# Token chunks of 128 for the second mixer's value products, and one early load of w_sg

## The chip, the cores and the metric

The kernel runs on one core of one Trainium2 chip. The metric is device time in microseconds (us); before the change the median of three runs is 643.07 us (642.69 to 643.32). Names used below: PE is TensorE (matrix products), PEld the loading of its stationary operand ("weights"), DVE VectorE, ACT ScalarE, POOL GpSimd, SP the engine whose queue issues nearly all DMAs.

## The reference, cut to what matters

Two batches of 448 tokens with 768 channels pass through attention and two mixers. The change is in the second mixer, on whose input x it computes:

```python
h = x @ w_in                                   # 768 -> 1024
h = 0.5 * h * (1 + np.tanh(c * (h + 0.044715 * h ** 3)))
u, v = h[..., :512], h[..., 512:]
v_n = (v - mean(v)) / np.sqrt(var(v) + 1e-06) * g_ln      # over channels
v_s = np.einsum('ts,bsd->btd', w_sg, v_n) + b_sg[None, :, None]
return x + (u * v_s) @ w_out
```

The einsum mixes tokens: w_sg is 448 by 448, and the same for both batches. Before it stands the first mixer, a Fourier mix and a wide MLP (768 to 3072 to 768).

## The kernel before, in words

Every product that needs more than bf16 precision is done with operands split in a high and a low half (helper `split`: ACT copies the high half, DVE subtracts to get the low one), and three matrix instructions per block of 128 contracted rows: high by high, high by low, low by high. The helper `product` issues these, so one line, L140, holds nearly all of PE's work, and it is told apart by tiles: h and c are the first and second product of the MLP, u and v those with the two halves of w_in, sg the token mix with w_sg, out the product with w_out.

The MLP runs in six groups g = 0 to 5 of 512 hidden channels. In a group, h is computed for batch 0 and batch 1 (72 instructions each), then c for batch 0 and batch 1. Each group needs eight weight tiles, w1_(4g) to w1_(4g+3) and w2_(4g) to w2_(4g+3). They come as float64 words through one SP queue into two raw buffers (tag `raw`, 768 KB each), and ACT and DVE turn each into a high and a low half in about seven instructions. The trace leaves the digits before the underscore out: w_8 is w1_8 as well as w2_8. Tiles w1_4 and w1_5 lie in a pool of their own, `wc`, which is closed when group 1's h products have been written down.

From group 1 on a scheduler sets the order on each engine: it takes instructions of all program parts as their inputs are expected, so that parts written one after another are interleaved, and then each engine runs its list strictly in that order.

Products with one result of up to 512 columns take their PSUM bank from `one_ps`, a ring of four banks. So the c product that is four places later waits for the DVE to have read the earlier one.

w_sg is needed transposed and split, as sgT. Before, this is done in group 3 (L1145 to L1152): four tiles of 112 rows each are loaded into one buffer, one after another (`bufs=1`), transposed on PE in four pieces of 112 by 112, and split. The tokens are thus in four chunks of 112 (CP = 112, NT = 4).

After the last group follow u for batch 0, v for batch 0, u for batch 1, sg for batch 0, v for batch 1, out for batch 0, sg for batch 1, out for batch 1. `gate_values` computes v: for each chunk of 112 tokens the tokens are the stationary operand (128 contracted rows by 112 columns) and 256 columns of w_in stream past; 36 instructions a chunk, 144 a batch. Each chunk then goes through the tanh form of gelu, a norm over its 512 channels, and a split into vn. `gate` contracts the chunks of vn with sgT: four chunks, three instructions each, for each of four blocks of 128 channels.

Of the kernel before, what the change touches and what calls it, by code (L numbers as in the profile page):

```python
# [21 lines left out]
P = 128  # L22
# [2 lines left out]
NP = H // 2  # L25
CP = S // 4
NT = 4
FF1 = 4 * C
NF = FF1 // P
NG = 6  # L30
# [60 lines left out]
def attention_mixers_kernel(ctx, tc, bounded, q, k, v, cap, w_ch1, w_ch2, w_in, g_ln, w_sg, b_sg, w_out,  # L91
# [76 lines left out]

    xT = [keep.tile([P, NP, S], F32, name=f"xT{b}") for b in range(B)]
    normed = [None, None]  # L170


    def fourier(b, fp, t2sb, pool_folds=()):
# [83 lines left out]
    def layer_norm(b, fp):  # L257

        u = xT[b]

        def channel_sum(half, src, tag):
            vec.tensor_tensor(half, src[0], src[1], op=ALU.add)
            acc = fp.tile([P, S], F32, tag="acc", name=f"acc_{tag}{b}")
            vec.tensor_tensor(acc, half[:, 0, :], half[:, 1, :], op=ALU.add)
            vec.tensor_tensor(acc, acc, half[:, 2, :], op=ALU.add)
            return acc

        t = SimpleNamespace(d=[], sq=[])

        def total():  # L270
            half = fp.tile([P, 3, S + 2], F32, tag="y", bufs=2, name=f"half{b}")[:, :, :S]
            t.acc = channel_sum(half, (u[:, 0:3, :], u[:, 3:6, :]), "m")

        def mean():
            t.mu = two_ps(f"mu{b}", 1)[0]
            pe.matmul(t.mu[:, :S], mean_w, t.acc, start=True, stop=True)

        def centre():
            for i in range(2):
                d = fp.tile([P, 3, S], F32, tag="d", bufs=2, name=f"d{b}_{i}")  # L280
                vec.tensor_tensor(d, u[:, 3 * i:3 * i + 3, :], t.mu[:, :S].unsqueeze(1).to_broadcast([P, 3, S]),
                                  op=ALU.subtract)
                t.d.append(d)

        def square():
            for i in range(2):
                q2 = fp.tile([P, 3, S + 2], F32, tag="y", bufs=2, name=f"sq{b}_{i}")[:, :, :S]
                act.activation(q2, t.d[i], AF.Square)
                t.sq.append(q2)

        def square_total():
            t.acc2 = channel_sum(t.sq[0], t.sq, "v")

        def variance():
            t.vps = two_ps(f"var{b}", 1)[0]
            if bounded and not b:
                stream(t.vps, 12)
            for i in range(NT):
                pe.matmul(t.vps[:CP, 2 * i:2 * i + 2], t.acc2[:, i * CP:(i + 1) * CP], mean_w[:, 0:2],
                          start=True, stop=True)  # L300

        def deviation():
            var = small.tile([CP, NT], F32, tag="var", name=f"varc{b}")
            vec.tensor_scalar(var, t.vps[:CP, 0:2 * NT:2], 1e-6, None, op0=ALU.add)
            t.rstd = small.tile([CP, NT], F32, tag="rstd", name=f"rstd{b}")
            pool.tensor_tensor(t.rstd, var, neg_half[:CP, :NT], op=ALU.pow)

        def row():
            t.rps = two_ps(f"rstdrow{b}", 1)[0]
            if bounded and b:  # L310
                stream(t.rps, 12)
            for i in range(NT):
                pe.matmul(t.rps[:, i * CP:(i + 1) * CP], t.rstd[:, i:i + 1].to_broadcast([CP, P]), ident[:CP, :CP],
                          start=True, stop=True)

        def scale(c):
            part = lambda c: t.d[c // 3][:, c % 3, :]
            if c == 0:
                un[b] = normed[b].tile([P, 2, NP, S], F32R, tag="normed", name=f"un{b}")
            if c < NP:  # L320
                vec.tensor_tensor(part(c), part(c), t.rps[:, :S], op=ALU.mult)
            if 0 < c <= NP:
                act.copy(un[b][:, 0, c - 1, :], part(c - 1))
            if c > 1:
                vec.tensor_tensor(un[b][:, 1, c - 2, :], part(c - 2), f32(un[b][:, 0, c - 2, :]), op=ALU.subtract)  # L325

        return SimpleNamespace(total=total, mean=mean, centre=centre, square=square, square_total=square_total,
                               variance=variance, deviation=deviation, row=row, scale=scale)
# [466 lines left out]
    def gate_values(b, gp, x2, wv):  # L795

        vn = []

        def normalise(t, gv, mv):
            tc.keep_in_program_order(  # L800
                vec.tensor_scalar(gv, gv, mv[:, 0:1], mv[:, 1:2], op0=ALU.subtract, op1=ALU.mult))
            w = hpool[b].tile([P, 2, 512], F32R, tag="h", bufs=4, name=f"vn{b}_{t}")[:CP]
            split(w[:, 0], w[:, 1], gv)
            vn.append(w)

        last = None
        for t in range(NT):
            ps = one_ps(f"v{b}_{t}")
            for j in range(2):
                product(ps[:CP, j * 256:(j + 1) * 256], lambda n, a: x2[:, a, n, t * CP:(t + 1) * CP],  # L810
                        lambda n, a: wv[2 * j + n // 3][:, a, n % 3, :], NP)
            gv = gp.tile([P, DH], F32, tag="gv", bufs=3, name=f"gv{b}_{t}")[:CP]
            gelu2(gp, gv, ps[:CP, :], CP, f"v{b}_{t}", last)
            st = small.tile([P, 6], F32, tag="bst", name=f"bst{b}_{t}")[:CP]
            vec.bn_stats(st, gv)
            mv = small.tile([P, 2], F32, tag="bag", name=f"bag{b}_{t}")[:CP]
            vec.bn_aggr(mv, st)

            vec.tensor_scalar(mv[:, 1:2], mv[:, 1:2], 4e-6, None, op0=ALU.add)  # L819
            pool.tensor_tensor(mv[:, 1:2], mv[:, 1:2], neg_half[:CP, 0:1], op=ALU.pow)  # L820
            last = functools.partial(normalise, t, gv, mv)
        last()
        return vn
# [11 lines left out]
    def gate(b, gp, vn, ug, sgT, g_half, b_half):  # L835
        gated = normed[b].tile([P, 2, ND, S], F32R, tag="normed", name=f"gated{b}")
        for d in range(ND):
            ps = one_ps(f"sg{b}_{d}")
            product(ps[:, :S], lambda n, a: vn[n][:, a, d * P:(d + 1) * P], lambda n, a: sgT[:, a, n, :], NT)
            tmp = gp.tile([P, S], F32, tag="gelu", bufs=3, name=f"gate{b}_{d}")  # L840
            vec.scalar_tensor_tensor(tmp, ps[:, :S], g_half[:, d:d + 1], b_half, op0=ALU.mult, op1=ALU.add)
            vec.tensor_tensor(tmp, tmp, ug[d], op=ALU.mult)
            split(gated[:, 0, d, :], gated[:, 1, d, :], tmp)
        return gated
# [279 lines left out]
    if not bounded:  # L1124
        run(mixed(1, 0, hs1, w2, None))
    sp_pool = ctx.enter_context(tc.tile_pool(name="spatial", bufs=1, side="right"))
    sgT = sp_pool.tile([CP, 2, NT, S], F32R, name="sgT", bufs=1)
    g_half = sp_pool.tile([P, GATE_ROW // 4], F32, name="g_half", bufs=1)[:, :ND]
    b_half = sp_pool.tile([P, S], F32, name="b_half", bufs=1)
    x2 = [None] * B  # L1130
    for g in range(1, NG):
        if g == 1:
            if bounded:
# [6 lines left out]
        else:  # L1140
            w1 = [columns(w_ch1, g * GF + f, "w1_") for f in range(GF)]
            hs = [[], []]
            for b in range(B):
                run(hidden(b, g, un, w1, hs[b]))
        if g == 3:  # L1145
            for c in range(NT):
                sg_raw = sp_pool.tile([P, S], F32, tag="sgraw", bufs=1, name=f"sg_raw{c}")[:CP]
                sp.dma_start(sg_raw, w_sg[c * CP:(c + 1) * CP, :])
                ps = one_ps(f"sgT{c}")
                for t in range(NT):  # L1150
                    pe.transpose(ps[:CP, t * CP:(t + 1) * CP], sg_raw[:, t * CP:(t + 1) * CP], ident[:CP, :CP])
                src = ps[:CP, :S].rearrange("p (t x) -> p t x", t=NT)  # L1152
                split(sgT[:, 0, :, c * CP:(c + 1) * CP], sgT[:, 1, :, c * CP:(c + 1) * CP], src)
            sp.dma_start(g_half, g_ln.rearrange("(n p) -> p n", p=P))
            vec.tensor_scalar_mul(g_half, g_half, 0.5)
            sp.dma_start(b_half, b_sg.unsqueeze(0).to_broadcast([P, S]))
            vec.tensor_scalar_mul(b_half, b_half, 0.5)
        w2 = [rows(w_ch2, g * GF + f, "w2_") for f in range(GF)]
        for b in range(B):
            if g == NG - 1:  # L1160
                x2[b] = normed[b].tile([P, 2, NP, S], F32R, tag="normed", name=f"x2_{b}")
            run(mixed(b, g, hs[b], w2, x2[b]))

    gp = ctx.enter_context(tc.tile_pool(name="gating", bufs=2, side="right"))
    wu = [columns(w_in, d, "wu") for d in range(ND)]
# [2 lines left out]
    for j in range(2):  # L1168
        for k in range(2):
            block = w_in[k * HC:(k + 1) * HC, 2 * DH + j * 512:2 * DH + (j + 1) * 512]  # L1170
            w = weight(f"wv{j}{k}", block.rearrange("(k p) f -> p k f", p=P), 3, 256, "wb")
            wv.append(w.rearrange("p a (k f) -> p a k f", k=3))
    vn0 = gate_values(0, gp, x2[0], wv)
    ug1 = gate_inputs(1, gp, x2[1], wu)
    gated0 = gate(0, gp, vn0, ug0, sgT, g_half, b_half)
    vn1 = gate_values(1, gp, x2[1], wv)
    wo = [rows(w_out, d, "wo", "wa") for d in range(ND)]
    tail = project(0, gated0, wo, 3)
    run(tail, NP)
# [37 lines left out]
```

## Time and profile before

| what | us |
|---|---|
| median of three runs | 643.07 |
| lowest and highest run | 642.69, 643.32 |
| span of the profiled execution | 641.1 |
| PE busy within it | 621.4 |
| PEld busy | 536.5 |
| DVE busy | 502.7 |

The span goes from the first to the last instruction of the profiled execution. What lies around it is not in the profile's page; the median of the timed runs is 1.97 us above the span. PE's busy time has modelled ends, so that the start of one instruction to the start of the next is the better measure of what it costs; the chain of waits is counted that way.

### The profile page before, as it was taken

What the parts mean: (1) busy time and instruction counts of PE and PEld (TensorE: products, weight loads), DVE (VectorE), ACT (ScalarE), POOL (GpSimd) and SP (SyncE); (2) the same over time, 40 slices, a digit from 0 to 9 for tenths busy, and PEclk for the clock granted to TensorE, in tenths of its full rate; (3) what the DMA queues carried; (4) which work ended last, traced back from release to release, by engine and by line L of the source; (5) the groups of instructions that cost most, each with busy time, mean ns of one, the idle gap of its engine ahead of it and who ended that gap; (6) DMA issues with size and microseconds to landing.
All of it is one profiled execution on the core that took longest, in us unless ns stands there. A gap on an engine that the chain in (4) does not pass through costs nothing.

```text
span 641.1 us, 8759 instructions
## 1 busy us (share of the span) xinstructions
PE 621.4 (97%) x3414; PEld 536.5 (84%) x3414; DVE 502.7 (78%) x733; ACT 273.5 (43%) x374; POOL 82.9 (13%) x82
## 2 busy tenths in 40 slices
PE   7899999999999999999999999999999999999995
PEld 5444576559988999999999989999999999999995
DVE  1899999989985789998957882698589789997451
ACT  3998875671312244333403530352245244533121
POOL 1555564353000000000000000000000000101000
PEclk9999999999999999999999999999999999999998
DMA  6754820400401144544522360145054214000123
GB/s 164 185 135 102 244 61 15 139 0 2 147 2 28 50 147 154 174 157 138 167 99 70 128 204 32 48 151 173 23 153 143 99 50 149 1 1 1 44 58 78
DMA packets 69618, 62.74 MB, mean 98 GB/s; under 512 B 35840, under 2 KB 63296, under 8 KB 69568
## 3 DMA queue, kind: packets, MB, share of 16 engines
q1 hardware_dynamic: 68640, 61.86, 31.9%
q8 instruction: 29, 0.48, 0.3%
q10 hardware_dynamic: 928, 0.23, 0.2%
q14 instruction: 21, 0.17, 0.1%
HBM read 59.32 MB, written 2.75 MB: 97 GB/s over the span
## 4 chain that ended last, share of the span: by engine, by line
PE 83%; DVE 10%; DMA 2%; ACT 2%; issue 1%; POOLq 0%; POOL 0%; DVEq 0%; ACTq 0%; SPq 0%
PE c L140 26%; PE h L140 24%; PE v L140 5%; PE out L140 5%; PE u L140 4%; PE s L532 4%; PE o L556 4%; PE sg L140 3%; DVE r L576 2%; PE st L242 1%; DMA sg_raw<-in_moe_w_sg 1%; PE st L221 1%; PE tr L501 1%; ACT e L537 1%; PE idle L152 1%
## 5 line engine op out<-in xcount | busy, mean ns | idle before, releaser
L140 PE MATMUL h<-un,w 128*128 128x448 f32 x864 | 175.3, 363 | 0.5 <-DVE un L325 0.5
L140 PE MATMUL c<-h,w 128*128 128x448 f32 x864 | 175.4, 363 | 0.0
L140 PEld LDWEIGHTS h<-un,w 128*128 128x128 f32 x864 | 161.7, 188 | 12.4 <-DVE un L325 0.8
L140 PEld LDWEIGHTS c<-h,w 128*128 128x128 f32 x864 | 161.9, 188 | 11.1 <-issue 0.4
L736 DVE TENSOR_TENSOR xT<-xT,c 128x448 f32<-128x448 f32 x60 | 36.9, 617 | 37.2 <-PE c L140 37.2
L820 POOL TENSOR_TENSOR bag<-bag,neg_half 112x1 f32<-112x1 f32 x8 | 6.0, 745 | 396.5 <-DVE bag L819 396.5
L537 ACT ACTIVATE e<-s,tanh_scale 128x896 f32<-128x896 f32 (+1 forms) x48 | 41.1, 921 | 19.6 <-PE s L532 19.2
L556 PE MATMUL o<-e,v 128*64 128x448 f32 x192 | 41.1, 551 | 0.0
L541 ACT ACTIVATE e<-e,cap_pos 128x1792 f32<-128x1792 f32 (+1 forms) x24 | 37.7, 1620 | 0.0
L140 PE MATMUL v<-wv,x 128*112 128x256 f32 x288 | 34.2, 280 | 0.0
L140 PEld LDWEIGHTS v<-wv,x 128*112 128x112 f32 x288 | 34.1, 175 | 0.1
L727 ACT ACTIVATE h<-h 128x448 fp32r<-128x448 f32 x40 | 21.7, 542 | 28.7 <-DVE h L728 19.8
L532 PE MATMUL s<-qT,kT 64*128 64x448 f32 x216 | 27.5, 383 | 6.3 <-DVE qT L510 5.2
L576 DVE RECIPROCAL r<-den 128x448 f32<-128x448 f32 x11 | 32.4, 2948 | 0.8 <-PE den L569 0.7
L532 PEld LDWEIGHTS s<-qT,kT 64*128 64x128 f32 x216 | 19.3, 185 | 16.1 <-DVE qT L510 6.9
L140 PE MATMUL out<-gated,wo 128*128 128x448 f32 x144 | 30.8, 367 | 0.0
L140 PE MATMUL u<-x,wu 128*128 128x448 f32 x144 | 29.1, 362 | 0.0
L548 POOL TENSOR_TENSOR t<-t,e 128x896 f32<-128x896 f32 x12 | 28.6, 2381 | 0.8
L140 PEld LDWEIGHTS u<-x,wu 128*128 128x128 f32 x144 | 27.0, 188 | 1.8
L545 POOL TENSOR_TENSOR t<-e 128x896 f32<-128x896 f32 x12 | 27.8, 2320 | 2.7 <-POOL mix L521 1.7
L140 PEld LDWEIGHTS out<-gated,wo 128*128 128x128 f32 x144 | 26.4, 188 | 1.8 <-ACT res L861 0.2
L556 PEld LDWEIGHTS o<-e,v 128*64 128x64 f32 x192 | 11.8, 136 | 17.6 <-issue 15.2
(380 smaller groups left out, 900.7 us busy)
## 6 DMA issues: line engine op xcount, KB each, us to landing
k<-in_k SPq DMA_DIRECT2D x24, 112.0 KB, 2.8
out<-res SPq DMA_DIRECT2D x12, 224.0 KB, 2.5
q<-in_q SPq DMA_DIRECT2D x22, 112.0 KB, 2.8
t<-dft_channels SPq DMA_DIRECT2D x8, 291.0 KB, 5.1
v<-in_v SPq DMA_DIRECT2D x24, 96.0 KB, 2.3
w_0raw<-in_moe_w_ch SPq DMA_DIRECT2D x2, 768.0 KB, 5.0
w_1raw<-in_moe_w_ch SPq DMA_DIRECT2D x2, 768.0 KB, 6.0
w_2raw<-in_moe_w_ch SPq DMA_DIRECT2D x2, 768.0 KB, 4.7
```

The costliest lines, as they stand in the source:

```text
L140: pe.matmul(ps, lhs(i, a), rhs(i, b), start=start and m == 0, stop=stop and m == last)
L152: pe.matmul(ps[:, 0:2 * P], idle[:, 0:P], idle, start=True, stop=True)
L221: pe.matmul(ps[:HS, m * 256:m * 256 + NE], fold[:, i, m * HS:(m + 1) * HS], tab[:, i, :], start=i == 0, stop=i == 2)
L532: pe.matmul(ps[:, i, :S], t[lo:hi, x, at:at + P], qT[lo:hi, y, :], start=m == 0, stop=m == 2)
L537: act.activation(es[n][:, 2 * step:2 * step + nr], sums.pop((n, step))[:, :nr, :S], AF.Tanh, scale=tanh_scale)
L541: act.activation(part, part, AF.Exp, scale=cap_pos)
L545: pool.tensor_tensor(t, es[n][:, 0:2], es[n][:, 2:4], op=ALU.add)
L548: pool.tensor_tensor(ts[n], ts[n], es[n][:, 4:6], op=ALU.add)
L556: pe.matmul(os[n][halfs[j], :S], vts[n % 3][:, j, i], es[n][:, 2 * i + j if i < 3 else 6], start=i == 0, stop=i == 3)
L576: vec.reciprocal(r, den[:, :S])
L727: act.activation(h[:, 0], ps[:, i, :S], AF.Relu)
L736: vec.tensor_tensor(u[:, c, :], u[:, c, :], ps[:, :S], op=ALU.add)
```

## The change

The value products take the tokens in chunks of 128 (NB = 3 full chunks of a batch, and 64 tokens left over). The 64 left-over tokens of both batches share one chunk: the input tile of batch 0 is widened from 448 to 512 tokens a row (EXT), two POOL copies bring batch 1's last 64 tokens into it, and batch 0 computes four chunks, batch 1 three. The fourth chunk of vn is used by both batches. For that sgT gets five blocks of 128 rows instead of four of 112: three for the full chunks, and one for each batch's half of the shared chunk, in which the other batch's rows are zero. The loaded rows of w_sg stand in one tile for all four row blocks, widened by zero columns (a POOL memset), and are loaded in group 2 by two DMAs; the transposes stay in group 3 and become 20, of 112 rows by 128 columns. The tile's pool `sg_rows` lies where `wc` lay. In the module's last function the scratch for DMAs that software describes is made smaller.

```diff
+NB = S // P
+EXT = NB * P + P
...
+    def tokens(b, name):
+        t = normed[b].tile([P, 2, NP, S if b else EXT], F32R, tag="normed", name=f"{name}{b}")
+        wide[name, b] = t
+        return t[:, :, :, :S]
...
-        for t in range(NT):
+        for t in range(NB if b else NB + 1):
             ps = one_ps(f"v{b}_{t}")
             for j in range(2):
-                product(ps[:CP, j * 256:(j + 1) * 256], lambda n, a: x2[:, a, n, t * CP:(t + 1) * CP],
+                product(ps[:, j * 256:(j + 1) * 256], lambda n, a: x2[:, a, n, t * P:(t + 1) * P],
                         lambda n, a: wv[2 * j + n // 3][:, a, n % 3, :], NP)
...
-            product(ps[:, :S], lambda n, a: vn[n][:, a, d * P:(d + 1) * P], lambda n, a: sgT[:, a, n, :], NT)
+            product(ps[:, :S], lambda n, a: vn[n][:, a, d * P:(d + 1) * P],
+                    lambda n, a: sgT[:, a, n + b if n == NB else n, :], NB + 1)
...
+        if g == 2:
+            raws_sg = ctx_sg.enter_context(tc.tile_pool(name="sg_rows", bufs=1))
+            sg_raw = raws_sg.tile([CP, NT, 4 * P + D], F32, name="sg_raw", bufs=1)
+            pool.memset(sg_raw[:, :, NB * P:], 0.0)
+            rows_sg = w_sg.rearrange("(c p) s -> p c s", c=NT)
+            sp.dma_start(sg_raw[:, :, :NB * P], rows_sg[:, :, :NB * P])
+            sp.dma_start(sg_raw[:, :, NB * P + D:NB * P + 2 * D], rows_sg[:, :, NB * P:])
         if g == 3:
-            for c in range(NT):
-                sg_raw = sp_pool.tile([P, S], F32, tag="sgraw", bufs=1, name=f"sg_raw{c}")[:CP]
-                sp.dma_start(sg_raw, w_sg[c * CP:(c + 1) * CP, :])
-                ps = one_ps(f"sgT{c}")
-                for t in range(NT):
-                    pe.transpose(ps[:CP, t * CP:(t + 1) * CP], sg_raw[:, t * CP:(t + 1) * CP], ident[:CP, :CP])
-                src = ps[:CP, :S].rearrange("p (t x) -> p t x", t=NT)
-                split(sgT[:, 0, :, c * CP:(c + 1) * CP], sgT[:, 1, :, c * CP:(c + 1) * CP], src)
+            for n, at in enumerate((0, P, 2 * P, NB * P + D, NB * P)):
+                ps = one_ps(f"sgT{n}")
+                for c in range(NT):
+                    pe.transpose(ps[:, c * CP:(c + 1) * CP], sg_raw[:, c, at:at + P], ident[:CP, :CP])
+                split(sgT[:, 0, n, :], sgT[:, 1, n, :], ps[:, :S])
+            ctx_sg.close()
...
+    for a in range(2):
+        pool.tensor_copy(wide["x2_", 0][:, a, :, S:EXT], x2[1][:, a, :, NB * P:])
...
-    vn0 = gate_values(0, gp, x2[0], wv)
+    vn0 = gate_values(0, gp, wide["x2_", 0], wv)
...
-    vn1 = gate_values(1, gp, x2[1], wv)
+    vn1 = gate_values(1, gp, x2[1], wv) + vn0[NB:]
```

The rows below are the lists that the scheduler made, of before first and then of the changed kernel, whose line numbers are its own. The first place is PE where sgT is made, between group 3's h products and its c products (h0_4_0 is group 4's first h product of batch 0, c0_3_1 group 3's second c product of batch 0). Before:

```order
L140 MATMUL h1_3_2_3031<-un1_1787,w1_15_2894 128x448 x18
L1151 MATMUL sgT0_3076<-ident_87,sg_raw0_3074 112x112 x4
L140 MATMUL h0_4_0_3370<-un0_1396,w1_16_3329 128x448 x13
L1151 MATMUL sgT1_3085<-ident_87,sg_raw1_3083 112x112 x4
L140 MATMUL h0_4_0_3370<-un0_1396,w1_16_3329 128x448 x5
L140 MATMUL h0_4_0_3370<-un0_1396,w1_17_3340 128x448 x3
L140 MATMUL c0_3_1_3172<-h0_3_0_2939,w2_12_3117 128x448 x3
```

Now:

```order
L142 MATMUL h1_3_2_3038<-un1_1787,w1_15_2901 128x448 x18
L1167 MATMUL sgT0_3081<-ident_87,sg_raw_2649 128x112 x4
L1167 MATMUL sgT1_3088<-ident_87,sg_raw_2649 128x112 x4
L1167 MATMUL sgT2_3095<-ident_87,sg_raw_2649 128x112 x4
L1167 MATMUL sgT3_3102<-ident_87,sg_raw_2649 128x112 x4
L142 MATMUL h0_4_0_3377<-un0_1396,w1_16_3336 128x448 x2
L1167 MATMUL sgT4_3109<-ident_87,sg_raw_2649 128x112 x4
L142 MATMUL h0_4_0_3377<-un0_1396,w1_16_3336 128x448
L142 MATMUL c0_3_0_3165<-h0_3_0_2946,w2_12_3124 128x448 x3
```

The four groups of transposes, which stood apart with other products between them, now stand together, and a fifth follows after two products.

The second place is SP's queue from the last weight load of group 1 (w2_7) into group 2 (w1_8 and on). Before:

```order
L670 DMA w2_6raw_2240<-in_moe_w_ch2 128x1536
L670 DMA w2_7raw_2251<-in_moe_w_ch2 128x1536
L670 DMA w1_8raw_2430<-in_moe_w_ch1 128x6x256
L670 DMA w1_9raw_2441<-in_moe_w_ch1 128x6x256
L670 DMA w1_10raw_2452<-in_moe_w_ch1 128x6x256
```

Now:

```order
L679 DMA w2_6raw_2240<-in_moe_w_ch2 128x1536
L679 DMA w2_7raw_2251<-in_moe_w_ch2 128x1536
L1161 DMA sg_raw_2649<-in_moe2_w_sg 112x4x384
L679 DMA w1_8raw_2430<-in_moe_w_ch1 128x6x256
L1162 DMA sg_raw_2649<-in_moe2_w_sg 112x4x64
L679 DMA w1_9raw_2441<-in_moe_w_ch1 128x6x256
```

The two loads of w_sg moved ahead of w1_8 and of w1_9; the four that stood in group 1 and group 3 are gone.

The third place is PE at the end of batch 1's value products (v1_2 is the third chunk; out0_0 the first product with w_out). Before:

```order
L140 MATMUL v1_2_4900<-wv10_4384,x2_1_4111 112x256 x9
L140 MATMUL v1_2_4900<-wv11_4395,x2_1_4111 112x256 x9
L140 MATMUL v1_3_4954<-wv00_4362,x2_1_4111 112x256 x9
L140 MATMUL v1_3_4954<-wv01_4373,x2_1_4111 112x256 x9
L140 MATMUL v1_3_4954<-wv10_4384,x2_1_4111 112x256 x9
L140 MATMUL v1_3_4954<-wv11_4395,x2_1_4111 112x256 x9
L140 MATMUL out0_0_5056<-gated0_4723,wo0_5015 128x448 x3
```

Now:

```order
L142 MATMUL v1_1_4855<-wv10_4393,x2_1_4118 128x256 x9
L142 MATMUL v1_1_4855<-wv11_4404,x2_1_4118 128x256 x9
L142 MATMUL v1_2_4909<-wv00_4371,x2_1_4118 128x256 x9
L142 MATMUL v1_2_4909<-wv01_4382,x2_1_4118 128x256 x9
L142 MATMUL v1_2_4909<-wv10_4393,x2_1_4118 128x256 x9
L142 MATMUL v1_2_4909<-wv11_4404,x2_1_4118 128x256 x9
L142 MATMUL out0_0_5011<-gated0_4732,wo0_4970 128x448 x3
```

The fourth chunk of batch 1 is gone, and each of the others has 128 stationary columns instead of 112 (the first number of a row's shape).

## Rows read from the trace of the kernel before

**Rows 1.** The page: span; busy us, share and instructions of each engine.

```profile
span 641.1 us, 8759 instructions
...
PE 621.4 (97%) x3414; PEld 536.5 (84%) x3414; DVE 502.7 (78%) x733; ACT 273.5 (43%) x374; POOL 82.9 (13%) x82
```

**Rows 2.** Chain that ended last, in order: start us, length us, what.

```profile
226.56 28.81 PE h L140 x144
...
532.36 16.92 PE v L140 x144
...
573.30 16.92 PE v L140 x144
590.22 9.61 PE out L140 x48
...
605.96 9.61 PE sg L140 x48
```

**Rows 3.** Value-product stretches: length, busy us (count) of PE, PEld, DVE, ACT, POOL; clock.

```profile
532.40:549.30 16.90, 16.90 (x145) 16.90 (x144) 16.01 (x31) 6.75 (x11) 1.32 (x2) 1.00 0.30 98
573.30:590.20 16.90, 16.90 (x145) 16.90 (x145) 13.23 (x27) 5.84 (x10) 1.51 (x2) 1.00 0.00 1
```

**Rows 4.** Timeline, 192 to 195 us: start, length, engine, line, operation.

```profile
192.00 0.77 PEld L299 LDWEIGHTS var<-mean_w,acc_v 128*112 128x112 f32 x7
...
192.72 1.47 PE L152 MATMUL rstdrow<-ident 128*128 128x256 bf16 x12
...
194.22 0.97 PEld L313 LDWEIGHTS rstdrow<-ident,rstd 112*128 112x128 f32 x8 [0.32 <-POOL rstd L306]
```

**Rows 5.** Groups of weight loads, 192 to 195.1 us: count, busy us, mean ns.

```profile
L313 PEld LDWEIGHTS rstdrow<-ident,rstd 112*128 112x128 f32 x8 | 1.0, 189 | 0.3 <-POOL rstd L306 0.3
L299 PEld LDWEIGHTS var<-mean_w,acc_v 128*112 128x112 f32 x7 | 0.8, 178 | 0.0
```

**Rows 6.** Groups, matrix products, 192 to 195.1 us.

```profile
L152 PE MATMUL rstdrow<-ident 128*128 128x256 bf16 x12 | 1.5, 272 | 0.0
```

**Rows 7.** Groups, matrix products, 370.53 to 381.46 us.

```profile
L140 PE MATMUL h<-un,w 128*128 128x448 f32 x23 | 5.4, 371 | 0.0
L140 PE MATMUL c<-h,w 128*128 128x448 f32 x17 | 4.0, 369 | 0.0
L1151 PE MATMUL sgT<-ident,sg_raw 112*112 112x112 f32 x16 | 2.3, 268 | 0.9 <-DMA sg_raw<-in_moe_w_sg 0.8
```

**Rows 8.** PE timeline of transposes of another stage, then of w_sg.

```profile
60.23 0.55 PE L501 MATMUL tr<-ident,k 112*128 112x112 f32 x4
60.62 0.55 PE L501 MATMUL tr<-ident,q 112*128 112x112 f32 x4
...
370.53 0.55 PE L1151 MATMUL sgT<-ident,sg_raw 112*112 112x112 f32 x4
```

**Rows 9.** DVE timeline, first split of a w_sg chunk.

```profile
371.92 0.61 DVE L132 TENSOR_TENSOR sgT<-sgT,sgT 112x448 fp32r<-112x448 f32 x1
```

**Rows 10.** SP timeline, load of w1_8 (the profile's w_8).

```profile
249.09 0.38 SPq L670 DMA_DIRECT2D w_8raw<-in_moe_w_ch  x1
```

**Rows 11.** ACT timeline, first use of that load.

```profile
253.60 0.93 ACT L685 ACTIVATE w_8cvt<-w_8raw 128x768 f32<-128x768 f32 x1 [2.10 <-DMA w_8raw<-in_moe_w_ch]
```

**Rows 12.** DVE timeline, first addition of the second products.

```profile
259.30 0.61 DVE L736 TENSOR_TENSOR xT<-xT,c 128x448 f32<-128x448 f32 x1
```

**Rows 13.** POOL groups, whole span.

```profile
L545 POOL TENSOR_TENSOR t<-e 128x896 f32<-128x896 f32 x12 | 27.8, 2320 | 2.7 <-POOL mix L521 1.7 <-ACT e L541 0.5
...
L899 POOL MEMSET mix<- 128x256 f32 x2 | 0.6, 311 | 0.0
```

**Rows 14.** DVE timeline: last split of x2, gated0 and vn1.

```profile
519.86 0.62 DVE L132 TENSOR_TENSOR x<-xT,x 128x448 fp32r<-128x448 f32 x1
...
576.83 0.62 DVE L132 TENSOR_TENSOR gated<-gate,gated 128x448 fp32r<-128x448 f32 x1 [0.63 <-ACT gated L131]
...
597.89 0.69 DVE L132 TENSOR_TENSOR vn<-gv,vn 112x512 fp32r<-112x512 f32 x1 [0.69 <-ACT vn L131]
```

More of the change, by code (lines that the diff above doesn't have):

```diff
@@ L170, in attention_mixers_kernel @@
     normed = [None, None]
+    wide = {}
+    def tokens(b, name):
+        t = normed[b].tile([P, 2, NP, S if b else EXT], F32R, tag="normed", name=f"{name}{b}")
+        wide[name, b] = t
+        return t[:, :, :, :S]
     def fourier(b, fp, t2sb, pool_folds=()):
@@ L318, in scale @@
             if c == 0:
-                un[b] = normed[b].tile([P, 2, NP, S], F32R, tag="normed", name=f"un{b}")
+                un[b] = tokens(b, "un")
             if c < NP:
@@ L801, in normalise @@
                 vec.tensor_scalar(gv, gv, mv[:, 0:1], mv[:, 1:2], op0=ALU.subtract, op1=ALU.mult))
-            w = hpool[b].tile([P, 2, 512], F32R, tag="h", bufs=4, name=f"vn{b}_{t}")[:CP]
+            w = hpool[b].tile([P, 2, 512], F32R, tag="h", bufs=4, name=f"vn{b}_{t}")
             split(w[:, 0], w[:, 1], gv)
@@ L806, in gate_values @@
         last = None
-        for t in range(NT):
+        for t in range(NB if b else NB + 1):
             ps = one_ps(f"v{b}_{t}")
             for j in range(2):
-                product(ps[:CP, j * 256:(j + 1) * 256], lambda n, a: x2[:, a, n, t * CP:(t + 1) * CP],
+                product(ps[:, j * 256:(j + 1) * 256], lambda n, a: x2[:, a, n, t * P:(t + 1) * P],
                         lambda n, a: wv[2 * j + n // 3][:, a, n % 3, :], NP)
-            gv = gp.tile([P, DH], F32, tag="gv", bufs=3, name=f"gv{b}_{t}")[:CP]
-            gelu2(gp, gv, ps[:CP, :], CP, f"v{b}_{t}", last)
-            st = small.tile([P, 6], F32, tag="bst", name=f"bst{b}_{t}")[:CP]
+            gv = gp.tile([P, DH], F32, tag="gv", bufs=3, name=f"gv{b}_{t}")
+            gelu2(gp, gv, ps, P, f"v{b}_{t}", last)
+            st = small.tile([P, 6], F32, tag="bst", name=f"bst{b}_{t}")
             vec.bn_stats(st, gv)
-            mv = small.tile([P, 2], F32, tag="bag", name=f"bag{b}_{t}")[:CP]
+            mv = small.tile([P, 2], F32, tag="bag", name=f"bag{b}_{t}")
             vec.bn_aggr(mv, st)
             vec.tensor_scalar(mv[:, 1:2], mv[:, 1:2], 4e-6, None, op0=ALU.add)
-            pool.tensor_tensor(mv[:, 1:2], mv[:, 1:2], neg_half[:CP, 0:1], op=ALU.pow)
+            pool.tensor_tensor(mv[:, 1:2], mv[:, 1:2], neg_half[:, 0:1], op=ALU.pow)
             last = functools.partial(normalise, t, gv, mv)
@@ L1126, in attention_mixers_kernel @@
     sp_pool = ctx.enter_context(tc.tile_pool(name="spatial", bufs=1, side="right"))
-    sgT = sp_pool.tile([CP, 2, NT, S], F32R, name="sgT", bufs=1)
+    sgT = sp_pool.tile([P, 2, NB + B, S], F32R, name="sgT", bufs=1)
     g_half = sp_pool.tile([P, GATE_ROW // 4], F32, name="g_half", bufs=1)[:, :ND]
@@ L1130, in attention_mixers_kernel @@
     x2 = [None] * B
+    ctx_sg = ExitStack()
     for g in range(1, NG):
@@ L1160, in attention_mixers_kernel @@
             if g == NG - 1:
-                x2[b] = normed[b].tile([P, 2, NP, S], F32R, tag="normed", name=f"x2_{b}")
+                x2[b] = tokens(b, "x2_")
             run(mixed(b, g, hs[b], w2, x2[b]))
+    for a in range(2):
+        pool.tensor_copy(wide["x2_", 0][:, a, :, S:EXT], x2[1][:, a, :, NB * P:])
     gp = ctx.enter_context(tc.tile_pool(name="gating", bufs=2, side="right"))
@@ L1192 @@
     from concourse.bass_utils import run_bass_kernel_spmd
-    nc = bacc.Bacc("TRN2", target_bir_lowering=False, num_devices=1)
+    nc = bacc.Bacc("TRN2", target_bir_lowering=False, num_devices=1, dynamic_dma_scratch_size=1024)
     arrays, args = {}, []
```

## The prediction

> **What bounds the kernel.** I read the page first: PE is busy 621.4 of 641.1 us, DVE 78%, the rest less [rows 1]. PE's busy time has modelled ends, so I went on to the chain of waits in order of time: in both stretches of value products, and from group 1's h products on nearly everywhere, PE's own next instruction is the next step [rows 2]. The end moves with the sum of PE's start-to-start intervals, plus what PE waits. The changed instructions lie in three places: the value products (two stretches of 16.92 us, no wait in either), the transposes of w_sg, and the loads of w_sg on SP.
>
> **The value products.** Before, 288 instructions take 2 x 16.92 = 33.84 us, 117.5 ns each [rows 2]. After, seven chunks give 7 x 36 = 252. Each streams the same 256 columns, but its stationary operand has 128 columns instead of 112. So everything hangs on what sets the 117.5 ns: the stream, or the weight load beside it.
>
> PEld is busy all 16.90 us of either stretch [rows 3], which looks like a load bound. But busy means here only that loads overlap one another, since a load lasts longer than the interval at which loads start. Two spots at 192 to 195 us show that interval where little is streamed. Seven loads of 112 columns span 0.77 us and one lasts 178 ns: (0.77 - 0.178) / 6 = 98.7 ns. Eight loads of 128 columns span 0.97 us and one lasts 189 ns: (0.97 - 0.189) / 7 = 111.6 ns [rows 4, 5]. Between them stands a stream of 256 columns whose weights are bf16: twelve in 1.47 us, each 272 ns, so (1.47 - 0.272) / 11 = 108.9 ns [rows 4, 6]. So before, a 98.7 ns load runs beside a 108.9 ns stream and the pair costs 117.5, that is 8.6 ns over the longer one. With 128 columns the load comes to 111.6 ns and is the longer by 2.7 ns. No row shows this pair (split f32 operands, 128 stationary and 256 streamed columns), so I bound it:
>
> - Low end 117.5 ns: the load stays hidden as it is.
> - The 8.6 ns over the stream grow with the loaded columns: 8.6 x 128/112 = 9.8, so 118.7 ns. The h products say much the same: 28.81 / 144 = 200.1 ns for 448 columns and a 128-column load [rows 2], against 108.9 x 448/256 = 190.6, so 9.5 ns over.
> - The longer of the two plus the same 8.6: 120.2 ns.
> - High end: the load plus a tenth, 122.8 ns.
>
> I take 119.5, between the two middle ones. 252 x 0.1195 = 30.1 us, a gain of 3.7 us; by the ends 4.2 and 2.9.
>
> The Trainium skill ("Perfetto Trace Analysis", section "Identifying the Most-Contended Engine") says to judge TensorE's headroom by the busy share of its weight loads and not by that of its matmuls. By that rule these stretches are full of loads and bound by them; the loaded columns are the same before and after (288 x 112 = 252 x 128 = 32,256), so this term would be nothing. The trace agrees with the share, but its 98.7 ns speak against the conclusion; it is the first rival below.
>
> **The chunk's other work.** The eighth chunk's gelu, norm and split go from ACT, DVE and POOL. These engines are not waited for there, so I count nothing. What might be late next, now that out0 starts some 4 us earlier, at 586 instead of 590.22 [rows 2]: gated0's last split ends at 577.45, 8.5 us before. The last split of vn1 ended 8.4 us after the products (598.58 against 590.22), and sg1 starts 15.7 us after them (605.96) [rows 2, 14]; both distances stay. The token mix keeps its 96 instructions, which contract 128 rows instead of 112: 112 rows take 9.61 / 48 = 200.2 ns, h with 128 rows 200.1 [rows 2], so nothing.
>
> **The POOL copies.** Each moves 384 elements a partition; a POOL copy of 128 takes 292 ns [rows 13], so some 0.9 us each. They wait for x2's last split, which ends at 520.48 [rows 14], and are done by some 522.5. The list of waits has them ahead of the fourth chunk alone, not of u0; that chunk starts at 532.36 + 3 x 4.3 = 545.3. They are hidden with 22 us to spare. If u0 waited for them, it would cost about 5 us.
>
> **The transposes.** From 370.53 to 381.46 us PE starts 39 products (the 23 + 17 rows less one begun before), at 200 ns 7.8 us; so 16 transposes cost 10.93 - 7.8 = 3.1 us. A group of four takes 0.39 us in the shape that they have now (60.23 to 60.62), so 1.6 of it is transposing, 0.9 is idle, mostly for sg_raw's DMA, and 0.6 goes in four changes from one kind to the other [rows 7, 8]. After: five groups, 1.95 us, two changes, 0.3, and no DMA to wait for. The new wait is that of the fifth group, which needs the first one's bank. Its split ended at 372.53 [rows 9]; PE gets there at 370.53 + 1.56 + 2 x 0.2 = 372.5. So about 0; the products behind it find their banks some 2 us after their splits. Five groups cost 2.2 to 2.4 us, a gain of 0.8; ends 0.3 (a wait of half a microsecond) and 1.1.
>
> **The loads.** The first load of w_sg waits for the last reader of w1_5, the 108th h product of group 1: 226.56 + 108 x 0.2 = 248.2 us [rows 2]; behind it on SP stand w1_8 and all later weights. w1_8 was issued at 249.09 [rows 10], so the wait itself delays nothing. The second waits for the POOL memset, which waits for the same and takes about 0.9 us (768 columns at 311 ns for 256 [rows 13]): over at 249.3. But 672 KB now travel beside w1_8's 768 KB. w1_8 landed 4.5 us after issue, at 253.6 [rows 10, 11]; sharing evenly it lands at most 4.5 x 672/768 = 3.9 us later. Behind it on DVE stand the additions of the c products. The first one ended at 259.91, and its bank is needed by the fifth c product, which starts at 226.56 + 28.81 + 48 x 0.2 = 265.0 [rows 2, 12]. That is 5.1 us of cover, against 3.9. No cost; 1.2 us are left.
>
> The wider input tile and the smaller scratch change addresses only. Nothing, unless a stream slows with its row distance, which no row here shows.
>
> **The sum.** 3.7 + 0.8 = 4.5 us less: the span goes from 641.1 to 636.6. The median of the runs is 1.97 us above the profiled span, and I keep that: 643.07 - 4.5 = 638.6. Ends of this case: 4.2 + 1.1 = 5.3 (637.8) and 2.9 + 0.3 = 3.2 (639.9).
>
> **The rivals.**
> 1. The value products are bound by their loads. For: PEld has no gap in them [rows 3]. Then an instruction costs 117.5 x 128/112 = 134.3 ns, 252 of them 33.84 us as before, and only the transposes' 0.8 is left: 642.3. Against: loads of 112 columns start every 98.7 ns elsewhere [rows 4, 5]. 8%.
> 2. The load of w_sg stops group 1 on PE: w1_8 comes so late that DVE's additions hold the PSUM ring. It decides from 5.1 us of delay on, and turns the sum from 5.1 + 4.5 = 9.6 us on, when w1_8 takes 14.1 us instead of 4.5. At four times its time (18 us, 13.5 late) PE stands still for 8.4 us: 638.6 + 8.4 = 647.0. For: cover is short and the queue strictly in order. Against: the two transfers together are only 1.9 times the bytes. 3%.
> 3. Once the load is longer than the stream, the two stop overlapping: 111.6 + 108.9 = 220.5 ns, 55.6 us, so 643.07 + 21.7 - 0.8 = 664.0. It turns the sum above (33.84 + 0.8) / 252 = 137.5 ns. Against: the 128-column loads beside a stream of 112 columns keep their 111.6 ns [rows 4]. 2%.
> 4. The load leaves group 3, but PE gains nothing there, because the fifth group waits out what the DMA waits gave: 643.07 - 3.7 = 639.4, within the range. 7%.
>
> **How the numbers follow.** The forecast has 80%, rival 4 has 7%; both are faster by over 0.2% (1.29 us, about what a measurement of this kernel can tell from no change). Rival 1 (0.8 us) is within it, 8%. Rivals 2 and 3 are slower, 5%. The range is the forecast's own, 637.8 to 639.9, widened by the spread of the runs (642.69 to 643.32) and by a partial stop in group 1: 637.2 to 640.6. Left out are rivals 1 to 3, 13%, and a little of the forecast.
>
> **What would show it.** Right: 252 value products at 118 to 121 ns, in stretches of about 17.2 and 12.9 us; in group 3 five groups of transposes without a DMA in front, the fifth idle under 0.3 us; no idle PE at 255 to 285 us. Wrong: an interval near 134 ns (rival 1); additions behind w1_8 and PE idle near 265 us (rival 2); intervals above 137 ns (rival 3); a wait of PE on POOL at u0 or at the fourth chunk.

## The result, and the profile after

The changed kernel takes 637.26 us (median of four runs, 635.98 to 637.48); the kernel before took 642.88 beside it (641.09 to 643.32). The ratio is 0.9915, with a 95% interval of 0.9899 to 0.9932: 5.6 us less, where 4.5 were predicted, and just inside the predicted range of 637.2 to 640.6. The profiled execution took 637.37 us.

The page first: span, and per engine busy us, share and instructions, to be held beside [rows 1].

```profile
span 635.6 us, 8692 instructions
...
PE 617.2 (97%) x3382; PEld 532.8 (84%) x3382; DVE 499.2 (79%) x726; ACT 271.8 (43%) x372; POOL 84.1 (13%) x84
```

PE has 32 instructions less: 36 value products went and four transposes came. Its busy time fell by 4.2 us, the span by 5.5. The rest was idle time or is hidden in modelled ends, so the chain of waits is the view to go by. Chain of the changed kernel, in order of time: start us, length us, what.

```profile
226.61 28.81 PE h L142 x144
...
370.64 1.54 PE sgT L1167 x16
372.18 0.42 PE h L142 x2
372.60 0.53 PE sgT L1167 x4
...
516.78 14.41 PE u L142 x72
531.20 16.80 PE v L142 x144
...
572.02 12.72 PE v L142 x108
584.74 9.61 PE out L142 x48
...
600.50 9.61 PE sg L142 x48
```

Set against [rows 2], each landmark tells what had been gained by then: at the start of group 1's h nothing (226.61 against 226.56), at the first value products 1.16 us, at out0 5.48, at sg1 5.46. The end gives 5.5. So two places hold the whole gain: group 3 (from group 1's h to v0 it is 304.59 us, was 305.80: 1.21 us), and the value products (16.80 + 12.72 = 29.52 us, was 33.84: 4.32 us). Nothing is given back behind them: from out0 to sg1 15.76 us pass, against 15.74.

Value-product stretches of the changed kernel: length, then busy us (count) of PE, PEld, DVE, ACT, POOL, then the clock, DMA share, GB/s; the counterpart of [rows 3].

```profile
531.20:548.00 16.80, 16.80 (x145) 16.80 (x145) 15.98 (x32) 6.78 (x11) 1.21 (x2) 1.00 0.32 110
572.02:584.74 12.72, 12.72 (x109) 12.72 (x109) 9.61 (x19) 4.11 (x7) 0.82 (x1) 1.00 0.00 1
```

PEld is still full, and 16.80 / 144 = 116.7 and 12.72 / 108 = 117.8 ns are what 112 columns cost, 117.5. The loads got 16 columns wider and the products not a nanosecond longer.

PE timeline of the changed kernel around the transposes: start us, length us, engine, line, operation, shapes, count.

```profile
370.48 1.70 PE L1167 MATMUL sgT<-ident,sg_raw 112*128 112x112 f32 x16
371.95 0.65 PE L142 MATMUL h<-un,w 128*128 128x448 f32 x2
372.52 0.60 PE L1167 MATMUL sgT<-ident,sg_raw 112*128 112x112 f32 x4
372.90 0.45 PE L142 MATMUL h<-un,w 128*128 128x448 f32 x1
373.18 1.16 PE L142 MATMUL c<-h,w 128*128 128x448 f32 x5
```

Sixteen transposes run in one go, then the scheduler has put two h products before the last four. From 370.48 to 373.18 us three products take 0.6, so twenty transposes cost 2.1 us; the sixteen before cost 3.1, their waits for the DMA included [rows 7].

The tile's own view gives the fifth group's wait, and no DMA stands among what ended an idle time (tile sg_raw: shortest, median and longest duration in ns, then what its instructions waited for, us, times).

```profile
L1159 POOL MEMSET sg_raw<- x1: 742/742/742, 248.3 to 248.3; 112x768 f32 x1
...
  PE h L142: 54.1, 1
  DVE sgT L134: 0.3, 1
```

The 0.3 us is the fifth group's first weight load; PE itself shows no gap there, since the two h products fill the time. The 54.1 us is POOL's memset, which waits for the last reader of w1_5 and delays nobody.

### The profile page after: what moved, and what is told of

Read it like the earlier page. It is cut to its first block, busy times and chain, and to the rows that moved or that the text cites. A ratio compares the mean times of both kernels' runs of the same rounds, so it can differ in the third digit from the quotient of the medians.

```text
span 635.6 us, 8692 instructions
## 1 busy us (share of the span) xinstructions
PE 617.2 (97%) x3382; PEld 532.8 (84%) x3382; DVE 499.2 (79%) x726; ACT 271.8 (43%) x372; POOL 84.1 (13%) x84
## 4 chain that ended last, share of the span: by engine, by line
PE 84%; DVE 11%; ACT 2%; issue 1%; POOLq 0%; POOL 0%; DVEq 0%; ACTq 0%
PE c L142 26%; PE h L142 25%; PE v L142 5%; PE out L142 5%; PE u L142 5%; PE s L541 4%; PE o L565 4%; PE sg L142 3%; DVE r L585 2%; PE st L251 2%; PE st L230 1%; PE tr L510 1%; ACT e L546 1%; PE idle L154 1%; PE xt L869 1%
## 5 line engine op out<-in xcount | busy, mean ns | idle before, releaser
L1180 POOL CAST x<-x 128x384 fp32r<-128x384 f32 x2 | 1.3, 668 | 270.1 <-ACT x L133 269.6
L142 PEld LDWEIGHTS v<-wv,x 128*128 128x128 f32 x252 | 29.8, 188 | 0.1
L142 PE MATMUL v<-wv,x 128*128 128x256 f32 x252 | 29.8, 279 | 0.0
```

The lines of the kernel that those rows point to most:

```text
L142: pe.matmul(ps, lhs(i, a), rhs(i, b), start=start and m == 0, stop=stop and m == last)
```

## The experiments

Ten kernels were run. Four of them (the changed kernel again, the chunks alone, the early load alone, the doubled streams) were timed in five rounds on one chip beside the kernel before (642.06 us there). The other six ran once each and are read by their profile.

**The changed kernel again.**

> The changed kernel again, beside the three others, so that they can be compared with it on the same chip: 637.3 us, 29.5 us of value products.

Measured: 636.45 us, ratio to before 0.9911 (0.9896 to 0.9926), value products 16.80 and 12.72 us as above. It is the yardstick for the other three that were timed. Its profile is that of its slowest execution (638.42 us), and there PE has a wait that the first profile of this kernel doesn't show. Three pieces of its chain of waits (start us, length us, what), then PE's timeline at the end of them:

```profile
249.36 6.56 DMA w_8raw<-in_moe_w_ch
...
298.60 0.54 DVE h L737
...
299.19 14.68 PE h L142 x72
```

```profile
299.19 2.07 PE L142 MATMUL h<-un,w 128*128 128x448 f32 x9 [0.32 <-DVE h L737]
```

The chain runs back from the h products of group 2 over the conversions and loads of group 2's weights to block 8, which took 6.56 us beside w_sg's load; its own 4.5 us are in [rows 10, 11]. So the early load isn't free in every execution: here PE stood still for 0.32 us, and in the trace of the half loads (below) it has a similar wait of 0.14. The traces of the kernel before and of the chunks alone, with w_sg loaded in group 3, show no such wait; whether those kernels have it in other executions isn't known.

**The chunks alone.**

```diff
-        if g == 2:
-            sg_raw = raws_sg.tile([CP, NT, 4 * P + D], F32, name="sg_raw", bufs=1)
-            sp.dma_start(sg_raw[:, :, :NB * P], rows_sg[:, :, :NB * P])
...
         if g == 3:
-            for n, at in enumerate((0, P, 2 * P, NB * P + D, NB * P)):
+            for c in range(NT):
+                sg_raw = sp_pool.tile([P, S], F32, tag="sgraw", bufs=1, name=f"sg_raw{c}")[:CP]
+                sp.dma_start(sg_raw, w_sg[c * CP:(c + 1) * CP, :])
...
+                for n in range(NB):
+                    pe.transpose(ps[:, n * CP:(n + 1) * CP], sg_raw[:, n * P:(n + 1) * P], ident[:CP, :CP])
+                pe.transpose(ps[:D, NB * CP:NT * CP], sg_raw[:, NB * P:], ident[:CP, :CP])
...
+            pool.tensor_copy(sgT[D:, :, NB + 1, :], sgT[:D, :, NB, :])
...
```

> The chunks of 128 tokens alone: w_sg comes as in the kernel before, in four tiles of 112 rows through one buffer in group 3, each transposed and split there. Theory (the two parts add up, value products 4.3 us, group 3 about 1.1 us of the 5.6): 252 value products at 117 ns, 29.5 us, group 3 as slow as before, so 638.4 us. Rival (the chunks carry all of the gain, and group 3's gain is given back later): 637.3 us. Second rival (the chunks gain only as predicted, at 119.5 ns, and the rest comes from the load): 639.4 us.

Measured: 637.79 us, ratio 0.9939 (0.9926 to 0.9953). Chain: start us, length us, what.

```profile
226.68 28.81 PE h L142 x144
...
532.22 16.80 PE v L142 x144
...
573.04 12.72 PE v L142 x108
```

The value products have their whole gain, and from group 1's h to v0 it is 305.54 us, of the 305.80 before. So without the early load only 0.26 of the 1.21 us is there; the rest comes with it. By the ratios the chunks gave 0.61% (3.9 us) of 0.89%. The median alone lies between the theory and the first rival; against the changed kernel beside it, it is 1.3 us slower, where the theory has 1.1 and that rival nothing. With the chain the theory holds: the first rival falls by the 305.54 us, the second by products at 117 ns.

**The early load alone.** The kernel before, with this:

```diff
...
+        if g == 2:
+            raws_sg = ctx_sg.enter_context(tc.tile_pool(name="sg_rows", bufs=1))
+            sg_raw = raws_sg.tile([CP, NT, S], F32, name="sg_raw", bufs=1)
+            sp.dma_start(sg_raw, w_sg.rearrange("(c p) s -> p c s", c=NT))
         if g == 3:
...
-                sg_raw = sp_pool.tile([P, S], F32, tag="sgraw", bufs=1, name=f"sg_raw{c}")[:CP]
-                sp.dma_start(sg_raw, w_sg[c * CP:(c + 1) * CP, :])
...
-                    pe.transpose(ps[:CP, t * CP:(t + 1) * CP], sg_raw[:, t * CP:(t + 1) * CP], ident[:CP, :CP])
+                    pe.transpose(ps[:CP, t * CP:(t + 1) * CP], sg_raw[:, c, t * CP:(t + 1) * CP], ident[:CP, :CP])
...
```

> The early load alone: token chunks of 112 as before, w_sg in one tile during group 2, and 16 transposes of 112 x 112 in group 3 with no transfer in front of them. Theory: group 3 gains the waits for the transfers, 0.9 us, and some changes of kind, together 1.1 to 1.4 us; value products stay at 117.5 ns, 33.8 us; so 641.5 to 641.8 us. Rival (the load beside the first weights of group 2 takes back what group 3 gains): 642.9 us, no change.

Measured: 641.08 us, ratio 0.9983 (0.9974 to 0.9992). Chain of this kernel.

```profile
227.10 28.81 PE h L140 x144
...
371.13 1.53 PE sgT L1154 x16
...
531.32 16.92 PE v L140 x144
...
572.26 16.92 PE v L140 x144
```

From group 1's h to v0 304.22 us, 1.58 less than before; the value products as before. That is more than the changed kernel's 1.21, which has four transposes more (0.53 us in its chain). In this trace the load beside group 2's weights takes nothing back. By the ratios 0.17% (1.1 us), and with the 0.61% of the chunks 0.78%, of 0.89% with both: the parts add up within their intervals.

**Half the loaded columns.**

```diff
-                product(ps[:, j * 256:(j + 1) * 256], lambda n, a: x2[:, a, n, t * P:(t + 1) * P],
+                product(ps[:D, j * 256:(j + 1) * 256], lambda n, a: x2[:, a, n, t * P:t * P + D],
...
```

> The changed kernel with 64 instead of 128 loaded columns in the value products: the second half of every chunk's tokens is left out. Theory (the load is hidden, and what an instruction costs over its stream doesn't come from it): the 252 products stay at 117 ns, 29.5 us. Rival (the prediction's: the time over the 108.9 ns stream grows with the loaded columns): 108.9 + 8.2 x 64/128 = 113 ns, 28.5 us.

The other half of every chunk is left out, so the result is not the kernel's. The stretches of value products, columns as above.

```profile
531.52:548.48 16.96, 16.96 (x145) 16.96 (x144) 16.14 (x32) 6.75 (x11) 1.21 (x2) 1.00 0.31 109
572.69:585.69 13.00, 13.00 (x110) 13.00 (x110) 9.26 (x18) 4.09 (x7) 0.53 (x1) 1.00 0.00 1
```

117.8 and 120.4 ns: half the load saves nothing (the second stretch even costs 2.6 ns more, which is not explained). The rival, which was the prediction's own reading of the 8.6 ns, falls. And PEld is full here too, with half the columns, because one load still lasts longer than the interval: the group's row (count, busy us, mean ns, idle before) has 134 ns, and that of the changed kernel, with 128 columns, 188.

```profile
L142 PEld LDWEIGHTS v<-wv,x 128*64 128x64 f32 x252 | 29.8, 134 | 0.4 <-issue 0.3
```

**Half the streamed columns.**

```diff
-                product(ps[:, j * 256:(j + 1) * 256], lambda n, a: x2[:, a, n, t * P:(t + 1) * P],
-                        lambda n, a: wv[2 * j + n // 3][:, a, n % 3, :], NP)
+                product(ps[:, j * P:(j + 1) * P], lambda n, a: x2[:, a, n, t * P:(t + 1) * P],
+                        lambda n, a: wv[2 * j + n // 3][:, a, n % 3, :P], NP)
...
```

> The changed kernel with value products of 128 columns instead of 256, so half of the columns is left out and filled by a copy on POOL; the loads are the same 252. Theory (loads of 128 columns start at best every 111.6 ns, and below that they set the interval): 111 to 113 ns, 28.3 us, 1.2 us less. Rival 1 (the stream alone sets it, and the loads could go faster): 128 x 0.456 = 58 ns, 14.7 us. Rival 2 (a load as long as the 117 ns interval is already the bound): 117 ns, 29.5 us.

```profile
531.26:547.29 16.03, 16.03 (x146) 16.03 (x145) 13.97 (x30) 5.43 (x11) 2.00 (x5) 1.00 0.35 117
571.36:583.37 12.01, 12.01 (x110) 12.01 (x109) 9.82 (x21) 3.86 (x9) 1.33 (x3) 1.00 0.00 1
```

16.03 / 144 = 111.3 and 12.01 / 108 = 111.2 ns, close to the 111.6 that [rows 4, 5] gave for loads of 128 columns. With the streamed columns halved the interval fell by 5% only, so these products have a floor near 111 ns, and at 256 columns they lie some 5 ns above it. Both rivals fall as they were stated.

That the 128 loaded columns set this floor is not shown. No run has few loaded and few streamed columns together, and the transposes speak against it: the changed kernel's sixteen, which load 128 columns and stream 112, start 1.54 / 16 = 96 ns apart (its chain above). Transposes of the output load 112 columns and stream 128; four of them in PE's timeline, and the durations of all 48 (tile xt, ns), are these.

```profile
594.19 0.60 PE L869 MATMUL xt<-ident,xT 128*112 128x128 f32 x4
```

```profile
L869 PE MATMUL xt<-ident,xT x48: 270/272/320, 594.2 to 628.9; 128*112 128x128 f32 x48
```

They start (0.60 - 0.272) / 3 = 109 ns apart. Among transposes the interval goes with the streamed columns (in a transpose these are as many as the contracted rows), not with the loaded ones. So a stream of 128 columns that is slow by itself stays a rival for the 111.3 ns.

**Twice the streamed columns.** A candidate to beat both kernels.

```diff
-            for j in range(2):
-                product(ps[:, j * 256:(j + 1) * 256], lambda n, a: x2[:, a, n, t * P:(t + 1) * P],
-                        lambda n, a: wv[2 * j + n // 3][:, a, n % 3, :], NP)
+            product(ps, lambda n, a: x2[:, a, n, t * P:(t + 1) * P], lambda n, a: wv[n][:, a, :DH], NP)
...
```

> The changed kernel with value products of 512 columns: 126 instructions instead of 252, the same result; w_in's half comes in six tiles of 128 rows instead of four. Theory (a product costs its stream and a constant, whatever is loaded): by 117.1 ns at 256 columns and 200.1 at 448 a column costs 0.432 ns and a product 6.5 ns beside, so 227.8 ns, 28.7 us, 0.8 us less than with 256 columns: 636.5 us. Rival (the share over the stream grows with the stream, so twice the columns cost twice the time, 234 ns): 29.5 us, 637.3 us, no change. Second rival (the first chunk now needs all six tiles at once and waits for the last): slower than 637.3 us, with PE idle before the first value product.

Measured: 637.90 us, ratio to before 0.9937 (0.9924 to 0.9951), against 0.9911 of the changed kernel beside it: by the medians 1.4 us slower than that. Its chain, and PE's timeline where v0 begins (idle before it in brackets).

```profile
536.25 13.37 PE v L142 x56
549.62 14.40 PE u L142 x72
...
573.64 12.59 PE v L142 x54
```

```profile
531.14 3.89 PE L142 MATMUL v<-wv,x 128*128 128x512 f32 x16
536.25 0.97 PE L142 MATMUL v<-wv,x 128*128 128x512 f32 x3 [1.22 <-ACT wv L133]
```

The theory of a constant part falls: 12.59 / 54 = 233.1 ns is twice 116.6, so what an instruction costs over its bare stream grows with the stream. The first rival has the size and the second the sign: 0.13 us gained in the undisturbed second stretch, and in the first stretch a wait of 1.22 us for the split of w_in's last tile, which here the first chunk already needs. Merging the products is not worth that; no version of these beats the changed kernel.

**What sets the share over the stream?** Three kernels built on the one with long streams, each with 448 columns, because products that load weights and stream 448 token columns take 200.1 ns (14.41 / 72, u above): the value products as they are, then with token columns streamed as well, then with w_in's columns both streamed and loaded. The first leaves out part of the value products' result, the other two all of it.

```diff
-            product(ps, lambda n, a: x2[:, a, n, t * P:(t + 1) * P], lambda n, a: wv[n][:, a, :DH], NP)
+            product(ps[:, :S], lambda n, a: x2[:, a, n, t * P:(t + 1) * P], lambda n, a: wv[n][:, a, :S], NP)
...
```

> The kernel of the long streams with 448 instead of 512 columns in each of its 126 value products (64 columns are left out and filled by a copy on POOL). In that kernel an undisturbed product took 233.1 ns, twice the 116.6 of 256 columns, so 0.455 ns a column, while all products that stream 448 token columns take 200.1 ns, 0.447 a column. Theory (the number of columns sets the time, and 448 is a size that streams better): 200 ns. Rival (the streamed operand sets it: rows of w_in stream slower than token columns): 448 x 0.455 = 204 ns.

> As the experiment with 448 columns, but the value products stream 448 token columns instead of 448 of w_in's (the loaded operand stays the token chunk; the value products' real result is left out). With w_in streamed the undisturbed product took 206 ns; products that load a weight and stream 448 tokens take 200.1. Theory (where the streamed operand lies sets the 6 ns): 200 ns, 1.5 us less over 252 half products or 126 whole ones x 6 ns = 0.8 us less. Rival (where the loaded operand lies sets them): 206 ns again.

> The counterpart: the value products stream 448 columns of w_in and also load 128 columns of w_in instead of the token chunk (their real result is left out). Theory (the streamed operand sets the 6 ns): 206 ns. Rival (the loaded operand does): 200 ns.

The second stretch of each, in which no product waited, from its chain: w_in streamed, then tokens in both operands, then w_in in both.

```profile
570.79 11.13 PE v L142 x54
```

```profile
569.37 11.16 PE v L142 x54
```

```profile
570.00 10.99 PE v L142 x54
```

206.1, 206.7 and 203.5 ns. So 448 columns are not a better size by themselves, and neither operand decides alone: tokens streamed with weights loaded cost 200.1, with tokens loaded 206.7, and w_in in both stands between. The expectation of the last two had one cause or the other; both fall. What in the pair of operands makes the 3% is open.

**Five times the load.**

```diff
+            spare = raws_sg.tile([CP, 4 * NT, NB * P], F32, name="spare", bufs=1)
+            sp.dma_start(spare, w_sg[:CP, :NB * P].unsqueeze(1).to_broadcast([CP, 4 * NT, NB * P]))
             sp.dma_start(sg_raw[:, :, :NB * P], rows_sg[:, :, :NB * P])
```

The transfer before block 8's was 2,688 KB by the trace (the expectation's 2,752 is the same size in thousands of bytes). The scheduler put the two loads of w_sg behind that of w1_9 (issued from 255.66 us on; block 8's load at 249.56), so nothing else new stands ahead of block 8.

> The changed kernel with 2,752 KB more on SP's queue, ahead of the load of w_1 block 8 in group 2 (the rows of w_sg again, into a tile that nobody reads). The changed kernel's 672 KB there put the first step on that block 1.9 us later (255.53 instead of 253.60 us). Theory (the queue is served in order, so the delay grows with the bytes ahead, and there are 5.1 us of cover): 1.9 x 2752/672 = 7.8 us later than before, PE idle 2.7 us near 265 us, and 640 us in all. Rival (transfers of a queue share evenly, so the block lands at most as late as twice its own 4.5 us): at most 4.5 us later, no idle PE, 637.3 us.

ACT's first use of the block in the changed kernel, then the same in this one; this one's added load (size, us from issue to landing); and a window of it (columns as in the stretches above).

```profile
255.53 0.92 ACT L694 ACTIVATE w_8cvt<-w_8raw 128x768 f32<-128x768 f32 x1 [0.21 <-DMA w_8raw<-in_moe_w_ch]
```

```profile
263.93 0.89 ACT L694 ACTIVATE w_8cvt<-w_8raw 128x768 f32<-128x768 f32 x1 [5.80 <-DMA w_8raw<-in_moe_w_ch]
```

```profile
spare<-in_moe_w_sg SPq DMA_DIRECT2D x1, 2688.0 KB, 13.1
```

```profile
265.00:275.00 10.00, 10.00 (x52) 9.37 (x51) 8.95 (x14) 3.36 (x4) 0.00 (x0) 1.00 0.65 174
```

The block is 10.3 us later than before [rows 11], 2.5 more than the theory said and far beyond the rival's 4.5. The added load was issued at 248.65 and landed 13.1 us later, at 261.8, and the block some 2 us behind it: the transfer ahead goes first, or nearly so. But PE has no idle time, and the run took 636.68 us. Both theories fall in part: delay as the one, price as the other. DVE's timeline says why; first the changed kernel, then this one.

```profile
259.48 0.61 DVE L745 TENSOR_TENSOR xT<-xT,c 128x448 f32<-128x448 f32 x1
260.01 0.95 DVE L702 SCALAR_TENSOR_TENSOR w_8cvt<-w_8raw,w_8cvt 128x768 uint32<-128x768 uint32 x1
...
261.35 0.61 DVE L745 TENSOR_TENSOR xT<-xT,c 128x448 f32<-128x448 f32 x1
```

```profile
258.71 0.61 DVE L745 TENSOR_TENSOR xT<-xT,c 128x448 f32<-128x448 f32 x1
260.65 0.62 DVE L745 TENSOR_TENSOR xT<-xT,c 128x448 f32<-128x448 f32 x1 [1.33 <-PE c L142]
263.05 0.62 DVE L745 TENSOR_TENSOR xT<-xT,c 128x448 f32<-128x448 f32 x1 [1.78 <-PE c L142]
264.85 0.56 DVE L697 TENSOR_SCALAR w_8cvt<-w_8cvt 128x768 f32<-128x768 f32 x1 [1.18 <-ACT w_8cvt L694]
```

The changed kernel has one addition before the conversions of block 8 are through; this one has three before they begin. The order on DVE is worked out again for each kernel, and it moved the late block behind the additions, so that they never stood behind it. What a late block costs with the order held fixed was not tried.

## Why the prediction was right, step by step

**The value products' size.** The step "119.5, between the two middle ones" was too high; its low end (117.5, load hidden) was the case. 252 products took 29.52 us instead of 30.1, so the term gave 4.3 instead of 3.7. The forecast's own sign, 118 to 121 ns, did not come: 116.7 and 117.8 did. What failed is the reading of the 8.6 ns over the stream as something that the load brings in. With 64, 112 and 128 loaded columns a 256-column product costs 117.8, 117.5 and 116.7 ns in the first stretch; with 512 streamed columns the interval doubles, and the surplus with it. So it goes with the stream and not with the number of loaded columns, and the bf16 rows, from which 108.9 ns came [rows 6], don't show it. The h products misled me: 9.5 ns over 190.6 looks like the same constant as 8.6 over 108.9. But they load weights and stream tokens; with the value products' own operands 448 columns cost 206.1, so 15.5 over.

**Which of load and stream bounds.** That the loads don't bound these products is shown by the half loads. The step "With 128 columns the load comes to 111.6 ns and is the longer by 2.7 ns" compared with a stream of 108.9 ns, while these products take 116.7 to 117.8; so the load was not the longer of the two. The 111.6 ns itself is no rule for loads of 128 columns: the transposes of [rows 8], which load 128, start 0.39 / 4 = 97.5 ns apart. What sets the 111.3 ns of the halved streams is open.

**Rival 1 (bound by the loads, 134.3 ns)** is refuted, by the changed kernel itself and again by the half loads. The Trainium skill ("Perfetto Trace Analysis", section "Identifying the Most-Contended Engine") names the busy share of its weight loads, beside the share of peak arithmetic that a kernel reaches, as what TensorE's headroom is judged by. Here the share of the loads is full with 64, 112 and 128 loaded columns alike, and the interval, 116.7 to 120.4 ns, doesn't fall with fewer columns; as a sign that loads bound these products, the trace doesn't agree with it.

**Rival 3 (no more overlap, 220.5 ns)** is refuted by the same 117 ns.

**The transposes.** Predicted 0.8 with ends 0.3 and 1.1; measured 1.21 us from group 1's h to v0, above the upper end. The DMA waits went as said; the fifth group's load waited 0.3 us, PE not. The size was off because the twenty transposes cost 2.1 us, not the 2.2 to 2.4 that I summed, and what is left, some 0.2 us, lies outside the stretch of transposes. Rival 4 (no gain there) falls; the kernel with the chunks alone shows what it would have been, 305.54 us.

**The loads.** Predicted no cost. The first profile of the changed kernel shows none; the second one has 0.32 us, by the mechanism of rival 2 on a small scale and later, in group 2's h products. The block came 1.9 us later, not the 3.9 of the bound. But the 5.1 us of cover, and with it the point at which rival 2 decides, rested on DVE's order of before. 10.3 us of delay cost PE nothing where the order changed with it. The forecast was right there to within 0.3 us, with a wrong margin. The memset's end was summed as 249.3 us; its terms give 249.1, and nothing rests on it.

**The POOL copies.** Two of 668 ns on average, estimated 0.9 us each, done at 520.45 us; no PE wait names them. Rows 13 holds the wrong line for this step: the 292 ns stand in the group of the copies at L521, which I meant to show and which is this.

```profile
L521 POOL CAST mix<-kT 64x128 fp32r<-64x128 f32 x12 | 3.5, 292 | 0.7
```

**The sum.** 4.3 + 1.2 = 5.5 us, the span's whole difference. Predicted 4.5: the value products gave 0.6 more and group 3 0.4 more. Both terms lie above their own upper ends (4.32 against 4.2, 1.21 against 1.1), and 637.26 us is below the 637.8 of the forecast itself; it is inside the range only since that was widened to 637.2 by the spread of the runs. The places, the direction and the fall of the rivals came out as reasoned; that the time still lies in the range is in part luck.

## What to carry to other kernels

A full row of weight loads says only that a load lasts longer than the interval; whether loads bound is seen by changing the loaded columns alone. The interval of loads in a place with little streaming is a hint at most: it was 111.6 ns for 128 columns in one place and 96 in another. Price a product from rows with the same operand type and the same pair of operands, and scale it by its streamed columns, before a surplus is put down to the load. Where a scheduler orders the work, cover read from the old order need not be a bound, since the new order may go around a later transfer.

## What the runs showed that was not expected

- What a split f32 product costs over its bare columns grows with the stream and depends on the pair of operands: with 448 columns 200.1, 203.5, 206.1 and 206.7 ns in four pairings, at a granted clock of 1.00.
- With 64 instead of 128 loaded columns the same products were not faster but slower by 1.1 and 2.6 ns.
- The two stretches of the changed kernel differ by 1.1 ns a product (116.7 and 117.8), before they did not (117.5 both). The first one's token tile is the wider one. Whether that is the reason wasn't tried.
- Transposes that load 128 columns and stream 112 start 96 ns apart, those that load 112 and stream 128 start 109 ns apart.
- 2,688 KB ahead in SP's queue made a 768 KB block 10.3 us later than in the kernel before, 672 KB 1.9 us: 3.8 and 2.8 us per 1,000 KB.
